# Chunk-end factors kept in a float32 tile and spread by small transfers, one padded v, and a new order, in a gated linear attention that feeds a two-layer MLP

## The chip, the cores and the metric

One core of one Trainium2 chip. The metric is device time in microseconds (us), the median of several runs. The profiler takes one execution apart. The engines are PE (TensorE: matmuls, with PEld for its weight loads), DVE (VectorE), ACT (ScalarE), POOL (GpSimd) and SP (SyncE, which here only issues transfers).

## The reference

The first half is a gated linear recurrence for 4 batches, 8 heads, 768 steps and head dimension 48; the second is a two-layer MLP on the result (3072 tokens, 384 to 2048 to 384).

```python
f = 1.0 / (1.0 + np.exp(-f_logit))
for t in range(S):
    state = f[:, :, t, :, None] * state + np.einsum('bhd,bhe->bhde', k[:, :, t], v[:, :, t])
    y[:, :, t] = np.einsum('bhd,bhde->bhe', q[:, :, t], state)
...
h = x @ w_in
g = np.maximum(0.01 * h, h)
return (g @ w_out).astype(np.float32)
```

## The kernel before

**Units and chunks.** The sequence is cut into 6 chunks of 128 steps, and the work into 12 units, each of 256 tokens. Units 0 to 3 are "paired": unit j holds chunks 0 and 1 of batch j, two neighbouring steps of one chunk pair in a row of 128. Units 4 to 11 hold one chunk (2, 2, 3, 3, 4, 4, 5, 5) of two batches each. The two halves of a unit are called a = 0 and a = 1.

**The steps of a unit**, by the short names that the order uses:

- `Lf Lk Lq Lv` load raw f, k, q, v (192 KB a half; in units 4 and on in runs of 48 floats), by SP's queue. `WI WO` load the MLP's weights in eight pieces each into raw buffers of units 4 and 5 that are still free, and `ci co` cast them to bfloat16.
- `ge gl` on ACT give log of the gate: exp into a tile `e`, then ln(1 + e) into `lf` (L233, L245).
- `cs` on PE sums `lf` over the steps of the chunk (a triangular matmul, L254, L255 in paired units, L262 in the others). The sum of the whole chunk is also wanted down the partitions, one value for each feature: eight matmuls per unit against a column of ones give it (L265; L259 with `half_ones` in paired units). The last chunk (units 10 and 11) needs none.
- `dec` on ACT makes three tiles from these sums: `em` = exp(+) for k, `at` = exp(-) for q, both bfloat16, and `end`, 4 columns in float32 (L273, L274, L276 or L279).
- `k`, `q` scale raw k by `em` and raw q by `at` (L285, on DVE or POOL). In paired units PE transposes them (`tk tq`, L319) and ACT or DVE copies them out (`ck cq`). In units 4 and on SP issues a DMA transpose for each (`xk xq`, L339), which waits until the scaling is done.
- `sc` scores (L355, L362), `mk` four masked copies on DVE (L372, L376), `mx` the mix with v and with the state of the earlier chunk (L393), `ms` its second part in paired units, `xt` copies the result out as input of the MLP.
- `v` casts raw v to bfloat16 (L291) and then copies 16 columns of each head once more into a tile `v2` (L297, L300), so that the mix has 32-column pieces that lie across two heads.
- `pt` (k times v), `sf` on DVE adds it to the float32 state, `sb` on POOL multiplies the state by `end` (L488) and casts it (L491). The state that `sb` of one unit gives is read by `mx` two units later.
- `up`: 6 matmuls of 256 columns (L499) and `pr` on ACT, the leaky relu (L504); 8 for each unit. `dn`: 4 matmuls of 384 columns (L520), 8 for each unit; `ob` copies out, `st` stores. The last unit's second half goes by half the columns (`dc`, L542).
- `F_n_cols` issues n matmuls of zeros (L97); `Z..` and `M..` clear tiles and make constants.

**What sets the order.** The function runs through a string of words such as `up_4_7@2` (step, unit, number, and after the @ its PSUM banks). Each engine takes its instructions in the order of the words and waits in that order; SP's transfers stand in it too. Eight PSUM banks are given out by hand. Raw buffers are six deep, so that unit j's loads wait for unit j-6.

Of the kernel before, what the change touches and what calls it, by code (L numbers as in the profile page):

```python
# [15 lines left out]
def kernel(  # L16
# [14 lines left out]
    C = 128  # L31
# [30 lines left out]
    es = tiles(2, [128, 2, H * D], FP32, "e")  # L62
# [27 lines left out]
    zeros = const.tile([128, 512], BF16, tag="zeros")  # L90
# [16 lines left out]
    def clear_v2(i, e):  # L107
        engine(e).memset(v2s[i][:, :, 1:3, :], 0.0)
# [88 lines left out]
    def load(x, queue=nc.sync):  # L197
        def go(j, a):
            if paired(j):
                h = slice(0, H) if a == 2 else slice(4 * a, 4 * a + 4)  # L200
                queue.dma_start(out=by_pair(raw(j, x))[:, h].rearrange("t h s d -> t h (s d)"),
                                  in_=srcs[x][j, h, 0:2 * C, :].rearrange("h (t s) d -> t h (s d)", s=2))
            else:
                c, h = units[j]
                nc.sync.dma_start(out=raw(j, x)[:, a],
                                  in_=srcs[x][2 * h + a, :, c * C:(c + 1) * C, :].rearrange("h t d -> t h d"))
        return go
# [14 lines left out]
    def decays(j, ts, a):  # L222
        t = ts[j % 2]
# [5 lines left out]
    def gate_e(j, a):  # L229
        e = es[j % 2]  # L230
        src = raw(j, "f").rearrange("t a h d -> t a (h d)")
        part = slice(a, a + 1) if a < 2 else slice(0, 2)
        nc.scalar.activation(e[:, part], src[:, part], AF.Exp, scale=-1.0)  # L233

    def gate_l(j, a):
        e = es[j % 2]
# [10 lines left out]
    def cs(j, a, bank):  # L247
# [15 lines left out]
        if chunk(j, a) < NCH - 1:  # L263
# [4 lines left out]
    def end_of(j):  # L268
        return ends[j % 4]

    def dec(j, a):
        t = banks[st[j]["cs", a]]
        nc.scalar.activation(ems[j % 2][:, a], t[:, 0:H * D], AF.Exp, scale=1.0)  # L273
        nc.scalar.activation(ats[j % 2][:, a], t[:, 0:H * D], AF.Exp, scale=-1.0)  # L274
        if paired(j):
            nc.scalar.activation(end_of(j)[:, :, 2 * a:2 * a + 2].rearrange("t i p -> t p i"),  # L276
                                 t[:, 384:388].rearrange("t (p i) -> t p i", i=2), AF.Exp, scale=-1.0)
        elif chunk(j, a) < NCH - 1:
            nc.scalar.activation(end_of(j)[:, a], t[:, H * D:H * D + P2], AF.Exp, scale=-1.0)  # L279

    def scale(x):
        def go(j, a, e):
            eng = nc.gpsimd if e else nc.vector
            to, by = (khs, ems) if x == "k" else (qhs, ats)
            eng.tensor_mul(heads(j, to[j % NR], a)[:, :, :, 0:D], raw_heads(j, x, a), decays(j, by, a))  # L285
        return go

    def cast_v(j, a, e):
        vb, v2 = vbs[j % 3], v2s[j % 3]
        eng = engine(e)  # L290
        eng.tensor_copy(out=heads(j, vb, a), in_=raw_heads(j, "v", a))  # L291
        if paired(j):
            p = slice(0, P2) if a == 2 else slice(2 * a, 2 * a + 2)
            src = by_pair(raw(j, "v")).rearrange("t (p j) s d -> t j s p d", j=2)
            dst = v2.rearrange("t (s p) n e -> t n s p e", s=2)
            for i in range(2):
                eng.tensor_copy(out=dst[:, 3 * i, :, p], in_=src[:, i, :, p, 32 - 32 * i:48 - 32 * i])  # L297
# [99 lines left out]
    def mix(j, a, *bank):  # L397
# [3 lines left out]
        vb, v2 = vbs[j % 3], v2s[j % 3]  # L401
        jobs = []
        if paired(j):
            halves = range(2) if a == 2 else (a,)
            for s in range(2):
# [7 lines left out]
                for g, which, p, y in todo:  # L413
                    for i in range(2):
                        rows = slice(64 * i, 64 * i + 64)
                        if which == "v":
                            lhsT = vb[rows, s, 2 * p + y, 16 * y:16 * y + 32]
                        else:
                            lhsT = v2[rows, P2 * s + p, 2 * y:2 * y + 2, :]
# [7 lines left out]
        for i in range(2):  # L427
            for y in range(2):
                for p in range(P2):
                    jobs.append((i, 3 * p + 2 * y, vb[:, i, 2 * p + y, 16 * y:16 * y + 32], wm_of(j, i, y)[:, p, :]))  # L430
                for p in range(P2):
                    jobs.append((i, 3 * p + 1, v2[:, P2 * i + p, 2 * y:2 * y + 2, :], wm_of(j, i, y)[:, p, :]))
# [24 lines left out]
    def state(j, a, *bank):  # L457
        kh, vb = khs[j % NR], vbs[j % 3]
        if paired(j):
            for i in range(2):  # L460
                st[j]["pt", i] = bank[i]
            for p in range(P2):
                for s in range(2):
                    for i in range(2):
                        rows = slice(64 * i, 64 * i + 64)
                        nc.tensor.matmul(banks[bank[i]][:, 96 * p:96 * p + 96], kh[rows, s, 2 * p:2 * p + 2, :],
                                         vb[rows, s, 2 * p:2 * p + 2, :], start=(s == 0), stop=(s == 1))
            return
        st[j]["pt", a] = bank[0]
        for p in range(P2):  # L470
            nc.tensor.matmul(banks[bank[0]][:, 96 * p:96 * p + 96], kh[:, a, 2 * p:2 * p + 2, :],  # L471
                             vb[:, a, 2 * p:2 * p + 2, :], start=True, stop=True)

    def state_add(j, a):
        sf = sfs[batch(j, a)]
        pt = banks[st[j].pop(("pt", a))][:, 0:384].rearrange("t (p n) -> t p n", p=P2)
        for y in range(2):
            rows = slice(64 * y, 64 * y + 64)
            new = pt[rows, :, y * D:y * D + D]
            if chunk(j, a) == 0:  # L480
                nc.vector.tensor_mul(sf[rows], new, end_of(j)[rows, a, :, None].to_broadcast([64, P2, D]))  # L481
# [3 lines left out]
    def state_end(j, a):  # L485
        sf, sb = sfs[batch(j, a)], sbs[batch(j, a)][chunk(j, a) % 2]
        if chunk(j, a) > 0:
            nc.gpsimd.tensor_mul(sf, sf, end_of(j)[:, a, :, None].to_broadcast([128, P2, D]))  # L488
# [65 lines left out]
    def store_cols(j, a, h):  # L554
# [12 lines left out]
        "Af": load("f", nc.scalar), "Ak": load("k", nc.scalar), "WI": load_w_in, "WO": load_w_out, "ci": cast_w(w_in_b, 0), "co": cast_w(w_out_b, 8),  # L567
        "Zl": clear_pad(lfs), "Zk": clear_pad(khs), "Zq": clear_pad(qhs), "Zv": clear_v2, "Zb": clear_state,
# [109 lines left out]
```

## Time and profile before

| what | value |
|---|---|
| median of 3 runs | 178.74 us (178.73 to 179.76) |
| the profiled execution's own time | 178.47 us |
| its span, first to last instruction | 176.7 us |
| PE busy | 169.3 us, 96% of the span |
| ACT, DVE, POOL busy | 108.8, 80.3, 77.1 us |
| moved by DMA | 34.44 MB, mean 195 GB/s |

How to read it: a matmul's row has its length with its latency, while PE starts the next one long before that; what PE pays for a piece is read from the chain of waits, where pieces follow each other. A row of the chain has its start, its length and its line. A row of the timeline has start, length, engine, line and operation, with the idle time before it and what ended that in brackets; "SPq" is the time that SP's queue took to issue a transfer. A group's row ends with its count, its busy time in us and the mean of one in ns.

### The profile page before, as it was taken

To read this page: it belongs to the slowest core of one execution; us is meant where nothing else is said; L and a number is where in the kernel's file an instruction comes from. 1 tells how busy PE (TensorE), PEld (TensorE's weight loads), DVE (VectorE), ACT (ScalarE), POOL (GpSimd) and SP (SyncE) were. 2 spreads that over 40 slices of the span, in tenths; PEclk is the share of its full clock that TensorE was granted. 3 is DMA by queue.
4 is the path that set the end of the run, shared out by engine and by line. 5 is a ranking of instruction groups with operands and counts; after the bars stand their busy time and mean duration, and the time that the engine had idled before them with its cause. 6 is when DMAs were issued, how large, how long until landed. Compare 5 with 4: busy or idle time off the path is not lost.

```text
span 176.7 us, 5587 instructions
## 1 busy us (share of the span) xinstructions
PE 169.3 (96%) x2308; PEld 124.5 (70%) x2310; DVE 80.3 (45%) x170; ACT 108.8 (62%) x230; POOL 77.1 (44%) x141
## 2 busy tenths in 40 slices
PE   7698999999999999999999999999999999999993
PEld 2455798688676687767776688777776786788762
DVE  5799797943244644332215750191115843630020
ACT  3995749959846476865683368938882345237511
POOL 7388677540316535255550794274375570000000
PEclk9999999999999999999999999999999999999999
DMA  5999999979983979999999999999989987110013
GB/s 136 323 323 351 325 306 368 329 198 259 233 172 74 188 151 273 179 222 184 210 211 212 222 191 173 203 211 224 157 150 193 166 195 208 46 48 0 4 59 120
DMA packets 108329, 34.44 MB, mean 195 GB/s; under 512 B 101008, under 2 KB 107280, under 8 KB 108304
## 3 DMA queue, kind: packets, MB, share of 16 engines
q1 hardware_dynamic: 107248, 33.70, 82.6%
q10 hardware_dynamic: 1056, 0.39, 0.8%
q8 instruction: 18, 0.29, 0.7%
q14 instruction: 7, 0.06, 0.1%
HBM read 25.17 MB, written 4.72 MB: 169 GB/s over the span
## 4 chain that ended last, share of the span: by engine, by line
PE 87%; DVE 4%; ACT 2%; DMA 2%; issue 1%; POOL 1%; SPq 0%; DVEq 0%; POOLq 0%
PE ps L520 35%; PE ps L499 34%; PE ps L393 6%; PE ps L362 3%; DMA f_raw<-in_f_logit_dram 2%; DVE wm L372 2%; PE ps L319 2%; PE ps L262 2%; PE ps L542 2%; PE ps L355 1%; PE ps L471 1%; DVE kh L285 1%; ACT e L233 1%; PE ps L97 1%; ACT lf L245 1%
## 5 line engine op out<-in xcount | busy, mean ns | idle before, releaser
L504 ACT ACTIVATE gT<-ps 128x512 bf16<-128x512 f32 x96 | 53.1, 608 | 27.1 <-PE ps L499 26.7
L499 PE MATMUL ps<-xT,w_in 128*128 128x256 bf16 x576 | 69.6, 273 | 0.1
L520 PE MATMUL ps<-w_out,gT 128*128 128x384 bf16 x368 | 67.3, 326 | 0.0
L499 PEld LDWEIGHTS <-w_in 128*128 128x128 bf16 x576 | 55.1, 98 | 9.1 <-DVE xT L455 0.4
L520 PEld LDWEIGHTS <-gT 128*128 128x128 bf16 x368 | 34.4, 98 | 19.8
L285 POOL TENSOR_TENSOR qh<-q_raw,at 128x768 bf16<-128x768 f32 (+1 forms) x13 | 18.2, 1398 | 22.0 <-ACT end L279 6.9
L376 DVE TENSOR_TENSOR wm<-ps,ut 128x512 bf16<-128x512 f32 x32 | 20.1, 684 | 10.6 <-PE ps L362 10.5
L273 ACT ACTIVATE em<-ps 128x384 bf16<-128x384 f32 x24 | 11.9, 496 | 19.8 <-PE ps L265 9.3
L483 DVE TENSOR_TENSOR sf<-sf,ps 64x192 f32<-64x192 f32 x32 | 11.2, 349 | 18.0 <-PE ps L471 16.1
L491 POOL CAST sb<-sf 64x192 bf16<-64x192 f32 x40 | 14.5, 362 | 7.4 <-DVE sf L481 5.1
L285 POOL TENSOR_TENSOR kh<-k_raw,em 128x768 bf16<-128x768 f32 (+1 forms) x9 | 14.4, 1602 | 4.9 <-DMA q_raw<-in_q_dram 3.0
L291 POOL CAST vb<-v_raw 128x384 bf16<-128x384 f32 (+1 forms) x13 | 8.8, 676 | 17.3 <-DMA v_raw<-in_v_dram 16.6
L488 POOL TENSOR_TENSOR sf<-sf,end 128x192 f32<-128x192 f32 x16 | 9.1, 572 | 15.0 <-DVE sf L483 14.7
L531 DVE COPY osb<-ps 128x384 f32<-128x384 f32 x13 | 7.2, 554 | 16.1 <-PE ps L520 10.7
L233 ACT ACTIVATE e<-f_raw 128x384 f32<-128x384 f32 (+1 forms) x16 | 11.1, 695 | 2.1 <-DMA f_raw<-in_f_logit_dram 2.0
L372 DVE TENSOR_TENSOR wm<-ps,pair_mask 128x512 bf16<-128x512 f32 x16 | 10.4, 686 | 3.4 <-PE ps L355 3.0
L274 ACT ACTIVATE at<-ps 128x384 bf16<-128x384 f32 x24 | 11.9, 497 | 0.0
L245 ACT ACTIVATE lf<-e 128x384 bf16<-128x384 f32 (+1 forms) x16 | 10.9, 683 | 0.3
L455 DVE CAST xT<-ps 128x384 bf16<-128x384 f32 x11 | 6.1, 566 | 9.8 <-PE ps L393 9.5
L453 ACT CAST xT<-ps 128x384 bf16<-128x384 f32 x13 | 6.6, 526 | 5.5 <-PE ps L393 5.3
L529 ACT COPY osb<-ps 128x384 f32<-128x384 f32 x10 | 4.9, 493 | 6.9 <-PE ps L520 6.9
L97 PE MATMUL ps<-zeros 128*128 128x512 bf16 x20 | 7.8, 467 | 1.4 <-DVE zeros L93 1.2
(92 smaller groups left out, 158.2 us busy)
## 6 DMA issues: line engine op xcount, KB each, us to landing
q_raw<-in_q_dram SPq DMA_DIRECT2D x24, 192.0 KB, 3.8
v_raw<-in_v_dram SPq DMA_DIRECT2D x24, 192.0 KB, 3.6
f_raw<-in_f_logit_dram SPq DMA_DIRECT2D x23, 192.0 KB, 3.9
k_raw<-in_k_dram SPq DMA_DIRECT2D x23, 192.0 KB, 4.5
out_dram<-osb SPq DMA_DIRECT2D x23, 192.0 KB, 2.9
k_raw<-in_moe_w_in_dram SPq DMA_DIRECT2D x2, 384.0 KB, 5.4
f_raw<-in_moe_w_in_dram SPq DMA_DIRECT2D x2, 384.0 KB, 6.5
q_raw<-in_moe_w_in_dram SPq DMA_DIRECT2D x2, 384.0 KB, 6.6
```

Of the source, the lines that this page charges most:

```text
L233: nc.scalar.activation(e[:, part], src[:, part], AF.Exp, scale=-1.0)
L245: nc.scalar.activation(dst, src, AF.Ln, bias=1.0)
L273: nc.scalar.activation(ems[j % 2][:, a], t[:, 0:H * D], AF.Exp, scale=1.0)
L274: nc.scalar.activation(ats[j % 2][:, a], t[:, 0:H * D], AF.Exp, scale=-1.0)
L285: eng.tensor_mul(heads(j, to[j % NR], a)[:, :, :, 0:D], raw_heads(j, x, a), decays(j, by, a))
L372: nc.vector.tensor_mul(w.rearrange("t (s p) n -> t s p n", s=2), src.rearrange("t (s p n) -> t s p n", s=2, p=2), pair_mask[:, :, None, :] ...
L376: nc.vector.tensor_mul(w, src.rearrange("t (p n) -> t p n", p=P2), ut[:, None, :].to_broadcast([128, P2, 128]))
L483: nc.vector.tensor_add(sf[rows], sf[rows], new)
L491: nc.gpsimd.tensor_copy(out=sb[rows, :, y * D:y * D + D], in_=sf[rows])
L499: nc.tensor.matmul(pm[:, i, :], w_in_of(ff, kk), xT_of(j)[:, kk].rearrange("t a s -> t (a s)"), start=(kk == 0), stop=(kk == NK - 1))
L504: nc.scalar.activation(gT_of(j)[:, 2 * g:2 * g + 2, :], pm, AF.Prelu, alpha=0.01)
L520: nc.tensor.matmul(po, gT_of(j)[:, ff, 128 * a:128 * a + 128], w_out_b[ff // 2][:, ff % 2, :], start=(ff == 0), stop=(ff == NF - 1))
```

## The change

1. `at` becomes float32 and holds four more columns for each half, the exponentials of the chunk sums. In paired units one ACT instruction of 388 columns (L311) writes both, and the `end` instruction goes. The tiles `end` of these units are no more; `sf` and `sb` read the columns of `at`.
2. Units 4 to 9 (`SPREAD`) compute no chunk sums by matmul. The last row of their `at` already holds exp(-sum) for each feature, in one partition. Two small transfers for each unit on SP's queue (`xe`, L295; 48 runs of 8 floats each) bring it down the partitions into a tile `end`. For that, `at` of units 4 to 11 is laid out with the eight head pairs innermost: ACT writes and the scaling of q reads with a step of 16 floats.
3. The tile `e` is gone; the first exp is written over raw f.
4. `v` is cast once into a tile with heads padded to 80 columns, whose padding is zero; `v2` and its copies go.
5. The zero matmuls read a tile of 256 columns, twice for 512.
6. The whole order of words is another one, with other banks and other engines for some steps. It has 25 zero matmuls, 4 of them short (22 before), and the first two transfers of ACT's queue are f and v of unit 0 instead of f and k. Changes of shape between neighbouring steps on PE (full, score, mix, paired state) go from 55 to 52.

The diff, cut to its core:

```diff
-    ats = tiles(2, [128, 2, H * D], BF16, "at")
-    ends = tiles(4, [128, 2, P2], FP32, "end")
-    vbs = tiles(3, [128, 2, H, D], BF16, "vb")
-    v2s = tiles(3, [128, 2 * P2, 4, 16], BF16, "v2")
+    SPREAD = (4, 5, 6, 7, 8, 9)
+    ends = tiles(2, [128, 2, P2], FP32, "end")
+    ats = tiles(4, [128, 2 * (H * D + P2)], FP32, "at")
+    VW = D + 32
+    vbs = tiles(3, [128, 2, H, VW], BF16, "vb")
...
-        if chunk(j, a) < NCH - 1:
+        if chunk(j, a) < NCH - 1 and j not in SPREAD:
             for p in range(P2):
                 nc.tensor.matmul(t[:, H * D + p:H * D + p + 1], lf[:, a, 2 * p:2 * p + 2, :], ones_col,
...
+    def at_spread(j):
+        return ats[j % 4][:, 0:2 * H * D].rearrange("t (d y n) -> t n y d", y=2, d=D)
+    def spread_end(j, y):
+        nc.sync.dma_start(out=ends[j % 2][64 * y:64 * y + D].rearrange("d a p -> d (a p)"),
+                          in_=at_spread(j)[C - 1:C, :, y].rearrange("t n d -> t d n"))
...
     def dec(j, a):
         t = banks[st[j]["cs", a]]
         nc.scalar.activation(ems[j % 2][:, a], t[:, 0:H * D], AF.Exp, scale=1.0)
-        nc.scalar.activation(ats[j % 2][:, a], t[:, 0:H * D], AF.Exp, scale=-1.0)
-        if paired(j):
-            nc.scalar.activation(end_of(j)[:, :, 2 * a:2 * a + 2].rearrange("t i p -> t p i"),
-                                 t[:, 384:388].rearrange("t (p i) -> t p i", i=2), AF.Exp, scale=-1.0)
-        elif chunk(j, a) < NCH - 1:
-            nc.scalar.activation(end_of(j)[:, a], t[:, H * D:H * D + P2], AF.Exp, scale=-1.0)
+        if spread(j):
+            nc.scalar.activation(at_spread(j)[:, P2 * a:P2 * a + P2], t[:, 0:H * D].rearrange("t (p y d) -> t p y d", y=2, d=D),
+                                 AF.Exp, scale=-1.0)
+        else:
+            nc.scalar.activation(at_of(j)[:, a], t[:, 0:H * D + P2], AF.Exp, scale=-1.0)
...
     def cast_v(j, a, e):
-        eng.tensor_copy(out=heads(j, vb, a), in_=raw_heads(j, "v", a))
...
+        engine(e).tensor_copy(out=heads(j, vbs[j % 3], a)[:, :, :, 0:D], in_=raw_heads(j, "v", a))
```

Three places of the order show what moves. **PE, unit 4's chunk sums** (`cs_4_0`, `cs_4_1`; `lf` are the gate's logs, `ut` the triangle). Before:

```order
L262 LDWEIGHTS ut_159
L262 MATMUL ps2_147<-lf1_91,ut_159 128x384
L265 LDWEIGHTS lf1_91
L265 MATMUL ps2_147<-ones_col_156,lf1_91 128x1
...
L262 LDWEIGHTS ut_159
L262 MATMUL ps6_151<-lf1_91,ut_159 128x384
```

In the change:

```order
L268 LDWEIGHTS ut_154
L268 MATMUL ps7_147<-lf1_89,ut_154 128x384
L268 LDWEIGHTS ut_154
L268 MATMUL ps4_144<-lf1_89,ut_154 128x384
```

The four loads and four matmuls behind each sum are gone. **ACT, the first steps** (`f_raw0` is unit 0's f, `f_raw1` unit 1's; L332 and L356 copy transposes out). Before:

```order
L233 ACTIVATE e1_89<-f_raw1_65 128x384
L245 ACTIVATE lf1_91<-e1_89 128x4x2x48
L233 ACTIVATE e0_88<-f_raw0_64 128x384
L245 ACTIVATE lf0_90<-e0_88 128x4x2x48
L233 ACTIVATE e0_88<-f_raw0_64 128x384
L245 ACTIVATE lf0_90<-e0_88 128x4x2x48
L273 ACTIVATE em0_99<-ps1_146 128x384
L274 ACTIVATE at0_101<-ps1_146 128x384
L276 ACTIVATE end0_103<-ps1_146 128x2x2
```

In the change:

```order
L239 ACTIVATE f_raw0_64<-f_raw0_64 128x384
L251 ACTIVATE lf0_88<-f_raw0_64 128x4x2x48
L239 ACTIVATE f_raw0_64<-f_raw0_64 128x384
L251 ACTIVATE lf0_88<-f_raw0_64 128x4x2x48
L306 ACTIVATE em0_97<-ps0_140 128x384
L311 ACTIVATE at0_101<-ps0_140 128x388
L306 ACTIVATE em0_97<-ps1_141 128x384
L311 ACTIVATE at0_101<-ps1_141 128x388
L356 COPY kT0_108<-ps2_142 128x2x256
L356 COPY kT0_108<-ps3_143 128x2x256
L239 ACTIVATE f_raw1_65<-f_raw1_65 128x384
```

Unit 0 now goes first and alone; unit 1's gate comes behind unit 0's copies. **SP around unit 7's transposes** (`qh1`, `kh1` are unit 7's scaled q and k in both; `q_raw1` its raw q). Before, with its raw q loaded ten and nineteen transfers earlier:

```order
L339 DMA_TRANSPOSE kT0_113<-kh0_93 128x8x128
L205 DMA v_raw1_83<-in_v_dram 128x8x48
L339 DMA_TRANSPOSE qT1_116<-qh1_97 128x8x128
L339 DMA_TRANSPOSE kT1_114<-kh1_94 128x8x128
L535 DMA out_0_dram<-osb1_142 128x384
```

In the change:

```order
L212 DMA q_raw1_77<-in_q_dram 128x8x48
L557 DMA out_0_dram<-osb0_136 128x384
L295 DMA end0_99<-at2_103 48x1x8 x2
L212 DMA q_raw2_78<-in_q_dram 128x8x48
L557 DMA out_0_dram<-osb2_138 128x384
L212 DMA q_raw1_77<-in_q_dram 128x8x48
L212 DMA k_raw2_72<-in_k_dram 128x8x48
L557 DMA out_0_dram<-osb3_139 128x384
L295 DMA end1_100<-at3_104 48x1x8
L363 DMA_TRANSPOSE kT1_109<-kh1_92 128x8x128
L363 DMA_TRANSPOSE qT1_111<-qh1_95 128x8x128
```

The second half of unit 7's raw q is now loaded three transfers ahead of the first transpose, one of them small.

More of the change, by code (lines that the diff above doesn't have):

```diff
@@ L96, in fill @@
         for _ in range(n):
-            nc.tensor.matmul(banks[bank][:, 0:cols], zeros[:, 0:128], zeros[:, 0:cols], start=True, stop=True)
+            o, src = banks[bank][:, 0:cols], zeros
+            if cols > 256:
+                o, src = o.rearrange("t (a n) -> t a n", n=256), zeros[:, None, :].to_broadcast([128, cols // 256, 256])
+            nc.tensor.matmul(o, zeros[:, 0:128], src, start=True, stop=True)
     def engine(e):
@@ L266, in cs, with spread, at_of, end_of @@
                                  start=True, stop=True)
-    def end_of(j):
-        return ends[j % 4]
+    def spread(j):
+        return not paired(j) and (j in SPREAD or units[j][0] == NCH - 1)
+    def at_of(j):
+        return ats[j % 4].rearrange("t (a n) -> t a n", a=2)
+    def at_spread(j):
+        return ats[j % 4][:, 0:2 * H * D].rearrange("t (d y n) -> t n y d", y=2, d=D)
+    def end_of(j, a, rows=slice(0, 128)):
+        t = ends[j % 2][rows] if j in SPREAD else at_of(j)[rows, :, H * D:H * D + P2]
+        if paired(j):
+            t = t.rearrange("t a (n i) -> t a n i", i=2)[:, :, :, a]
+            return t[..., None].to_broadcast([rows.stop - rows.start, 2, 2, D])
+        return t[:, a, :, None].to_broadcast([rows.stop - rows.start, P2, D])
+    def spread_end(j, y):
+        nc.sync.dma_start(out=ends[j % 2][64 * y:64 * y + D].rearrange("d a p -> d (a p)"),
+                          in_=at_spread(j)[C - 1:C, :, y].rearrange("t n d -> t d n"))
+    def clear_ends(i, e):
+        engine(e).memset(ends[i], 0.0)
+    def like_end(j, t):
+        return t.rearrange("t (a n) d -> t a n d", a=2) if paired(j) else t
     def dec(j, a):
@@ L281, in scale @@
     def scale(x):
         def go(j, a, e):
-            eng = nc.gpsimd if e else nc.vector
-            to, by = (khs, ems) if x == "k" else (qhs, ats)
-            eng.tensor_mul(heads(j, to[j % NR], a)[:, :, :, 0:D], raw_heads(j, x, a), decays(j, by, a))
+            to, by = (khs, ems[j % 2]) if x == "k" else (qhs, ats[j % 4])
+            if x == "q" and spread(j):
+                assert a == 2
+                pairs = lambda t: t.rearrange("t a (p y) d -> t (a p) y d", y=2)
+                engine(e).tensor_mul(pairs(to[j % NR])[:, :, :, 0:D], pairs(raw(j, x)), at_spread(j))
+            else:
+                by = by if x == "k" else at_of(j)
+                engine(e).tensor_mul(heads(j, to[j % NR], a)[:, :, :, 0:D], raw_heads(j, x, a), decays(j, by, a))
@@ L400, in mix @@
             st[j]["py", i] = b
-        vb, v2 = vbs[j % 3], v2s[j % 3]
+        vp = pairs_of_v(vbs[j % 3])
         jobs = []
@@ L415, in mix @@
                         rows = slice(64 * i, 64 * i + 64)
[L416 to L419, printed above, removed]
+                        at = 96 * y if which == "v" else 32 + 32 * y
+                        lhsT = vp[rows, P2 * s + p, at:at + 32]
                         jobs.append((i, g, lhsT, wm_of(j, p // 2, y)[rows, 2 * s + p % 2, :]))
@@ L466, in state @@
                         nc.tensor.matmul(banks[bank[i]][:, 96 * p:96 * p + 96], kh[rows, s, 2 * p:2 * p + 2, :],
-                                         vb[rows, s, 2 * p:2 * p + 2, :], start=(s == 0), stop=(s == 1))
+                                         vb[rows, s, 2 * p:2 * p + 2, 0:D], start=(s == 0), stop=(s == 1))
             return
```

186 lines of the change are left out of this document (88 added, 98 removed).

## The prediction

> **What bounds the kernel now.** I read the page, then the stages, the chain, the timeline of the first 40 us, and SP's timeline.
>
> ```profile
> PE 169.3 (96%) x2308; PEld 124.5 (70%) x2310; DVE 80.3 (45%) x170; ACT 108.8 (62%) x230; POOL 77.1 (44%) x141
> DMA  5999999979983979999999999999989987110013
> ...
> 0.00:10.00 10.00, 7.09 (x48) 3.38 (x48) 6.88 (x25) 7.03 (x17) 5.93 (x27) 1.00 0.89 240
> 10.00:20.00 10.00, 9.03 (x222) 5.95 (x223) 8.80 (x18) 7.22 (x17) 7.58 (x19) 1.00 1.11 341
> ...
> 40.00:60.00 20.00, 20.00 (x235) 13.72 (x233) 8.54 (x20) 13.35 (x31) 6.09 (x9) 1.00 0.85 183
> 60.00:80.00 20.00, 20.00 (x306) 15.33 (x282) 8.77 (x17) 13.98 (x32) 8.81 (x15) 1.00 1.01 207
> ```
>
> From 40 us on PE (second number of a stage) never rests. So time is lost in two ways only: before 40 us, where units 0 to 2 pass from engine to engine and zero matmuls count as busy, and by any new wait later. The row "DMA" says that such a wait has a candidate: transfers are in flight nearly all the time up to about 145 us.
>
> **1. The sums by matmul.**
>
> ```profile
> 50.50 0.16 PE ps L262
> 50.67 0.08 PE ps L265 x4
> 50.75 0.18 PE ps L262
> ...
> 126.14 0.16 PE ps L262
> 126.30 0.66 PE ps L499 x6
> ```
>
> In the chain four L265 take 0.08 us, and a sum of the last chunk, which has none, is followed at once by the next work (126.30). Units 4 to 9 have 12 such groups, on PE, in its dense part: 12 x 0.08 = **-1.0**. It lies between 0.9 and 1.2, as the rows are rounded.
>
> **2. Changes of shape on PE.**
>
> ```profile
> 76.03 1.30 PE ps L520 x8
> 77.33 0.55 PE ps L362 x16
> 77.88 1.41 PE ps L520 x8
> ```
>
> Eight L520 behind a score take 1.41 instead of 1.30: 0.1 for each change of shape. 55 become 52: **-0.3** (-0.4 to 0, as some stand where PE waits anyway).
>
> **3. Work taken from ACT, DVE and POOL.** The `end` steps, the `v2` copies and one clear less are off the path while PE is dense: ACT is busy 13 to 14 of 20 us there, POOL 6 to 9. I cost it at nothing; PE's own work hides it. At the start it counts, below. Writing the first exp over raw f holds that buffer one step longer; its next load comes six units later: nothing.
>
> **4. The start, in the new order.** ACT now gates unit 0 alone, then makes its factors; unit 1 comes behind.
>
> ```profile
> 4.06 0.52 ACT L233 ACTIVATE e<-f_raw 128x384 f32<-128x384 f32 x1 [2.04 <-DMA f_raw<-in_f_logit_dram]
> 7.18 0.47 ACT L273 ACTIVATE em<-ps 128x384 bf16<-128x384 f32 x1
> ...
> 7.28 0.38 ACT em L273
> 7.66 0.38 ACT at L274
> 8.16 0.55 DVE qh L285
> 8.71 0.47 DVE kh L285
> 9.21 0.44 DVE qT L334
> ...
> 15.55 0.31 PE L393 MATMUL ps<-wm,vb 64*32 64x128 bf16 x16
> 26.25 2.79 ACT L504 ACTIVATE gT<-ps 128x512 bf16<-128x512 f32 x5 [0.92 <-PE ps L499]
> 30.19 2.48 DVE L372 TENSOR_TENSOR wm<-ps,pair_mask 128x512 bf16<-128x512 f32 x4 [0.48 <-PE ps L355]
> ```
>
> A walk along the queues with these lengths (rows of the chain are from start to start): gate of unit 0 from 4.06, two pairs at about 1.05, done 6.2; factors, four steps, done 7.9 (before, three pairs came first: 7.18 is the first factor). DVE: q, k, q, v, two copies, `sf`, four masks: done about 13.5, so unit 0's mix at 13.6 instead of 15.55. But unit 1 pays: its k on DVE stands behind these masks, POOL makes q, v and k of its second half one after the other (13.6 to 16.4), and its four masks, mixed with `sf` and a weight cast, end at about 22.2. Three `up` groups fill PE before its mix, where before there was one. Behind it the relus (2.79 for five, 0.56 each) pace PE up to the end of unit 2's mix, which I put at 36.6. PE has then done the work that the kernel before has done here:
>
> ```profile
> 37.07 0.25 PE L254 MATMUL ps<-lf,bu 128*128 128x192 bf16 x1
> 37.23 0.08 PE ps L254
> ```
>
> In both, 23.35 us at the chain's prices (0.65 for each `up` or `dn`, and so on: 15 `up` and 3 `dn` there, 14 and 4 here, all else alike). So **-0.6** (37.2 to 36.6). The walk has some 30 handovers; 0.05 us on each would take it to +0.9, and with unit 1's masks not in the way it could be -1.5.
>
> **5. The small transfers and what they stand among.** Their price has no row. The nearest small one is a 96 KB store:
>
> ```profile
> out_dram<-osb SPq DMA_DIRECT2D x2, 96.0 KB, 1.6
> q_raw<-in_q_dram SPq DMA_DIRECT2D x24, 192.0 KB, 3.8
> qT<-qh SPq DMA_TRANSPOSE x8, 3.8
> ...
> 174.07 0.33 SPq L557 DMA_DIRECT2D out_dram<-osb  x1
> ```
>
> So 1.6 to 3.8 to land and 0.33 (or less, or up to a load's 1 us) of SP's time; I take 0.3 for 48 short runs. `sb` waits for them, but `sb`'s result is read two units later, over 14 us on: hidden. What is not hidden is the queue:
>
> ```profile
> 55.89 1.23 SPq L339 DMA_TRANSPOSE kT<-kh  x1
> 57.21 0.53 SPq L205 DMA_DIRECT2D q_raw<-in_q_dram  x1
> ...
> 91.24 1.67 SPq L339 DMA_TRANSPOSE qT<-qh  x1
> 142.44 1.21 SPq L205 DMA_DIRECT2D v_raw<-in_v_dram  x2
> ...
> 99.91 0.55 PE ps L362 x16
> ```
>
> From 57.21 to 143.65 SP issues 54 loads, 13 transposes and 15 stores without a long rest. At 1.35 and 0.6 for the latter two that leaves 1.1 us for a load with SP's waits in it, about 1.0 without. Before, the transpose of unit 7's q was issued at 91.24, landed about 95.0, and the scores ran at 99.91. In the new order SP stops at unit 0's first store, then unit 4's q and k are scaled on POOL, and the second transpose issues at 58.6; then come 27 loads, 7 stores, 4 transposes and 6 small transfers up to the second half of unit 7's raw q: 58.6 + 27 + 4.2 + 5.4 + 1.8 = 97.0, landed 99.8. POOL's scaling follows, then the transpose:
>
> ```profile
> L285 POOL TENSOR_TENSOR qh<-q_raw,at 128x768 bf16<-128x768 f32 x8 | 13.2, 1651 | 18.2 <-ACT end L279 6.9 <-ACT at L274 4.1 <-ACT gT L504 2.9
> L488 POOL TENSOR_TENSOR sf<-sf,end 128x192 f32<-128x192 f32 x16 | 9.1, 572 | 15.0 <-DVE sf L483 14.7
> ```
>
> It now reads `at` in float32 with a step. Bounds: 1.65 as before, and 2.3 by the float32 product of L488 (572 x 4). 99.8 + 1.65 to 2.3 + 3.8 = 105.2 to 105.9. PE comes there after 91.4 us of its work (all steps ahead of it at the chain's prices), 13.2 behind (36.6 - 23.35): 104.6. Two places ahead are as tight by the same count: unit 4's scores (transpose landed 60.7, PE there at 60.3) and unit 5's `up`, whose relus stand behind four long gate steps: 0.3 each. So PE is at unit 7's scores at 105.2 and waits 0 to 0.7; I take 0.4. Together **+1.0**; 0 if loads go a little faster, 5 if they take 1.1 and the small transfers more.
>
> [...] No run here shows such a step; the row of 1651 is without one. ACT writes with the same step; its row is 0.38 and twice that would still be hidden, as ACT has 6 of 20 us free.
>
> **Sum**, against the profiled execution's 178.47 (span 176.7 and 1.8 around it): -1.0 - 0.3 - 0.6 + 1.0 = -0.9, so **177.6 us**. That execution is 0.3 below the median of the runs shown, 178.74.
>
> **Rivals.**
>
> - *The start gains more and the queue keeps up.* With -1.5 at the start and no wait: 178.47 - 1.0 - 0.3 - 1.5 = 175.7. For it: the first mix has two us in hand, and SP rests before unit 4 with loads done. Against: DVE and relus set the pace from 14 to 33 us in my walk.
> - *The transfers become the bound (slower).* One place decides: unit 7's raw q. If a load takes 1.1 us and a small transfer 0.5 of SP's time, it lands 2.7 + 1.2 = 3.9 later, and PE waits 0.4 + 3.9 there. With the other terms 178.47 - 1.9 + 0.6 + 4.3 = 181.5. From about 1.06 us a load the time is above that of before. For it: the row of DMA and 1.1 as the mean with waits; against: 1.1 counts SP's rests twice.
> - *The small transfers hold up the state.* `dec` of unit 8 overwrites `at` of unit 4 and so waits for its second small transfer, which stands behind a transpose on SP; ACT would stop, its relus too. By my count it has 1.5 us in hand; if it is 3 us late, 177.6 + 1.5 = 179.1.
> - *The order does nothing*: the start is as long as before and the waits come: 178.47 - 1.3 + 1.0 = 178.2.
>
> **How the numbers follow.** My sum and the last two rivals lie within 1% of the median, which is what a measurement of this kernel can tell from no change (176.95 to 180.5): 0.42 together. The first rival, with the part of my own case under 176.95: 0.35. The slow one, beyond 180.5: 0.23, as loads must go slower than they did without SP's rests. The range reaches from 175.2, half a us under the first rival, to 181.2, most of the way to the slow one; my own case alone is 176.6 to 178.9.
>
> **What would show it.** Right: no matmul against ones behind units 4 to 9; unit 0's mix before 14.5; PE at work without a break from about 24; POOL's q of units 4 and on at 1.65 to 2.3; unit 7's scores preceded by an idle PE of about 1 us or less, released by a DMA transpose. Wrong: a wait of over 2 us on PE behind 40 us, a first dense `up` later than 26, or PE's dense part no shorter than before.

## The result and the profile after

The change made the kernel slower by about 1%: 182.31 us (median of 20 runs, 179.71 to 183.85) against 179.35 for the kernel before, run beside it; the ratio is 1.0107, 95% interval 1.0076 to 1.0137. The ratio leaves out runs that lie over 1.5% above a kernel's fastest, so it is smaller than that of the medians. Two more measurements of the same change, below, gave 181.05 (1.0094) and 181.59 (1.0118).

The profiled execution took 182.88 us, with a span of 181.0 (before: 178.47 and 176.7). From its page, the engines' busy time, the granted clock, and the two groups with the step:

```profile
PE 171.3 (95%) x2265; PEld 125.1 (69%) x2265; DVE 78.7 (44%) x161; ACT 113.9 (63%) x211; POOL 77.8 (43%) x127
...
PEclk9999999999999999999999996999999999999999
...
L319 POOL TENSOR_TENSOR qh<-q_raw,at 128x768 bf16<-128x768 f32 x8 | 17.6, 2195 | 10.3 <-DMA q_raw<-in_q_dram 7.0
...
L308 ACT ACTIVATE at<-ps 128x384 f32<-128x384 f32 x16 | 13.5, 841 | 0.0
```

PE does less work than before (2265 matmuls for 2308) and is busy longer; one slice has a clock of 0.6. The scaling of q on POOL went from 1.65 to 2.2 us, ACT's write of `at` from 0.50 to 0.84.

The start came nearly as forecast. In the chain of waits the last piece of unit 2's mix ends at 36.7; the kernel before had done the same work on PE at 37.2, the row of L254 in the prediction:

```profile
35.70 1.02 PE ps L417 x73
36.73 5.35 PE ps L521 x48
...
77.46 0.60 ACT gT L526
78.06 0.13 SPq L295
...
83.98 3.52 DMA f_raw<-in_f_logit_dram
87.53 0.85 ACT f_raw L239
...
105.25 3.29 DMA qT<-qh
108.53 0.14 issue
108.67 0.62 PE ps L386 x16
109.29 5.01 PE ps L542 x20
```

In the kernel before, the chain stays on PE through the whole dense part. Here it leaves PE twice: from 77 to 95 it runs over a small transfer (L295) and SP's loads to unit 7's f, to ACT's gate and the relus behind it; and at 105.25 over a DMA transpose to unit 7's scores (L386). What PE waited for from 40 us on (in all, times, longest), and then the stretch around the second place: its length, the busy time of PE, PEld, DVE, ACT and POOL, the granted clock, DMA's share and GB/s:

```profile
PE ps L386 <- DMA qT<-qh: 1.9, 1, 1.9
PE ps L521 <- ACT gT L526: 0.5, 1, 0.5
PE ps L542 <- ACT gT L526: 0.3, 1, 0.3
```

```profile
104.00:108.00 4.00, 2.78 (x24) 2.01 (x21) 0.56 (x1) 3.72 (x8) 3.09 (x5) 1.00 0.66 124
108.00:110.00 2.00, 1.33 (x19) 0.91 (x20) 0.84 (x2) 0.88 (x2) 2.00 (x2) 0.80 0.99 191
110.00:112.00 2.00, 2.00 (x8) 0.91 (x6) 2.00 (x4) 0.00 (x0) 1.06 (x1) 0.50 1.14 226
112.00:114.00 2.00, 2.00 (x12) 1.11 (x11) 0.11 (x1) 0.00 (x0) 0.00 (x0) 0.85 1.20 246
```

From one matmul's start to the next, beyond the usual distance of its kind, PE loses 0.64 us at 89.0 and 0.43 at 94.2 (waits for relus) and 2.05 at 106.5 (the scores). The down matmuls behind that rest start 0.32 us apart instead of 0.16: the clock column gives 2 x (0.20 + 0.50 + 0.15) = 1.7 us lost.

SP's queue and POOL show why the scores waited. SP's rows (L212 a load, L295 small transfers, L363 a transpose), then POOL's scaling of unit 7's q:

```profile
96.22 1.18 SPq L295 DMA_DIRECT2D end<-at  x2
97.44 0.58 SPq L212 DMA_DIRECT2D q_raw<-in_q_dram  x1
98.12 0.52 SPq L557 DMA_DIRECT2D out_dram<-osb  x1
98.69 0.43 SPq L212 DMA_DIRECT2D q_raw<-in_q_dram  x1
...
102.50 1.28 SPq L363 DMA_TRANSPOSE kT<-kh  x1
105.25 1.23 SPq L363 DMA_TRANSPOSE qT<-qh  x1
```

```profile
103.03 2.19 POOL L319 TENSOR_TENSOR qh<-q_raw,at 128x768 bf16<-128x768 f32 x1 [5.76 <-DMA q_raw<-in_q_dram]
```

The second half of unit 7's raw q is issued at 98.69; POOL has waited 5.76 us for it when it starts at 103.03. A small transfer takes SP 0.6 us (1.18 for the pair above), as much as a load of 192 KB (0.58 and 0.43).

**The account** of the profiled executions, span for span: start -0.5; sums -1.24 (48 matmuls, 26 ns from start to start each); other prices of PE's work +0.4; rests +3.1; half clock +1.7; from PE's last matmul to the end 3.8 instead of 3.2, +0.55; the remaining 0.3 in small rests, 0.2 of it in unit 3's mix at 59.7. Together 4.3 = 181.0 - 176.7.

### The profile page after: what moved, and what is told of

It reads as the page before. It is cut to its first block, busy times and chain, and to the rows that moved or that the text cites. A ratio compares the mean times of both kernels' runs of the same rounds, so it can differ in the third digit from the quotient of the medians.

```text
span 181.0 us, 5487 instructions
## 1 busy us (share of the span) xinstructions
PE 171.3 (95%) x2265; PEld 125.1 (69%) x2265; DVE 78.7 (44%) x161; ACT 113.9 (63%) x211; POOL 77.8 (43%) x127
## 4 chain that ended last, share of the span: by engine, by line
PE 77%; DMA 6%; DVE 5%; ACT 5%; SPq 3%; issue 2%; POOL 0%; ACTq 0%; DVEq 0%
PE ps L521 32%; PE ps L542 30%; PE ps L417 5%; DMA f_raw<-in_f_logit_dram 4%; SPq L212 2%; PE ps L386 2%; DMA qT<-qh 2%; ACT gT L526 2%; PE ps L564 1%; PE ps L343 1%; PE ps L268 1%; DVE wm L396 1%; DVE qh L322 1%; PE ps L493 1%; DVE qT L358 1%
## 5 line engine op out<-in xcount | busy, mean ns | idle before, releaser
L521 PE MATMUL ps<-xT,w_in 128*128 128x256 bf16 x576 | 67.1, 273 | 0.6 <-ACT gT L526 0.5
L526 ACT ACTIVATE gT<-ps 128x512 bf16<-128x512 f32 x96 | 54.6, 607 | 17.8 <-PE ps L521 15.5
L319 POOL TENSOR_TENSOR qh<-q_raw,at 128x768 bf16<-128x768 f32 x8 | 17.6, 2195 | 10.3 <-DMA q_raw<-in_q_dram 7.0
L326 POOL CAST vb<-v_raw 128x384 bf16<-128x384 f32 (+1 forms) x9 | 6.8, 758 | 20.5 <-DMA v_raw<-in_v_dram 13.4
L308 ACT ACTIVATE at<-ps 128x384 f32<-128x384 f32 x16 | 13.5, 841 | 0.0
L510 POOL TENSOR_TENSOR sf<-sf,end 128x192 f32<-128x192 f32 x12 | 6.1, 506 | 16.4 <-DVE sf L505 10.1
L239 ACT ACTIVATE f_raw<-f_raw 128x384 f32<-128x384 f32 (+1 forms) x16 | 10.9, 690 | 3.6 <-DMA f_raw<-in_f_logit_dram 3.6
L251 ACT ACTIVATE lf<-f_raw 128x384 bf16<-128x384 f32 (+1 forms) x16 | 10.8, 682 | 0.4
L322 POOL TENSOR_TENSOR qh<-q_raw,at 128x384 bf16<-128x384 f32 x3 | 3.5, 1160 | 14.9 <-ACT at L311 14.9
L100 PE MATMUL ps<-zeros 128*128 128x512 bf16 (+1 forms) x25 | 8.5, 457 | 1.1 <-DVE zeros L93 1.1
```

The source lines that it names most:

```text
L239: nc.scalar.activation(e[:, part], e[:, part], AF.Exp, scale=-1.0)
L308: nc.scalar.activation(at_spread(j)[:, P2 * a:P2 * a + P2], t[:, 0:H * D].rearrange("t (p y d) -> t p y d", y=2, d=D), AF.Exp, scale=-1.0)
L319: engine(e).tensor_mul(pairs(to[j % NR])[:, :, :, 0:D], pairs(raw(j, x)), at_spread(j))
L322: engine(e).tensor_mul(heads(j, to[j % NR], a)[:, :, :, 0:D], raw_heads(j, x, a), decays(j, by, a))
L521: nc.tensor.matmul(pm[:, i, :], w_in_of(ff, kk), xT_of(j)[:, kk].rearrange("t a s -> t (a s)"), start=(kk == 0), stop=(kk == NK - 1))
L526: nc.scalar.activation(gT_of(j)[:, 2 * g:2 * g + 2, :], pm, AF.Prelu, alpha=0.01)
```

## Experiments

Ratios are to the kernel before, run beside each; the interval is 95%.

| kernel | median us | ratio | interval |
|---|---|---|---|
| q7_early | 180.38 | 1.0072 | 1.0038 to 1.0105 |
| g7_behind | 180.90 | 1.0097 | 1.0067 to 1.0127 |
| q7_g7 | 179.79 | 1.0044 | 1.0018 to 1.0069 |
| sums_back | 179.17 | 1.0003 | 0.9986 to 1.0020 |
| no_transfers | 179.30 | 1.0022 | 0.9995 to 1.0049 |
| transfers_unread | 179.57 | 1.0036 | 1.0003 to 1.0070 |
| old_order_sums | 179.45 | 1.0029 | 1.0002 to 1.0056 |
| old_order_spread | 184.30 | 1.0317 | 1.0258 to 1.0375 |
| change_again | 181.05 | 1.0094 | 1.0057 to 1.0131 |
| ends_on_act | 184.16 | 1.0297 | 1.0266 to 1.0327 |
| ends_on_act_v7 | 184.36 | 1.0300 | 1.0262 to 1.0339 |
| no_ends | 178.22 | 0.9972 | 0.9944 to 0.9999 |
| half_runs | 180.94 | 1.0097 | 1.0057 to 1.0137 |
| change_third | 181.59 | 1.0118 | 1.0087 to 1.0148 |
| act_stride | 178.76 | 0.9976 | 0.9954 to 0.9998 |
| sums_v7 | 178.63 | 0.9957 | 0.9937 to 0.9978 |

### Is it the place of the loads? q7_early, g7_behind, q7_g7

Words of the order; `Lq_7_1` loads half of unit 7's raw q, `ge_7 gl_7` are its gate steps on ACT.

```diff
-    q_6_2_1 xq_6 Lk_8_0 Lk_7_1 Lf_9_0 Lq_8_0 Lf_9_1 Lq_7_0
+    q_6_2_1 xq_6 Lq_7_1 Lk_7_1 Lf_9_0 Lq_7_0 Lf_9_1 Lq_8_0
...
-    up_5_6@1 pr_5_6 Lq_7_1 up_5_4@2
+    up_5_6@1 pr_5_6 Lk_8_0 up_5_4@2
```

> The changed kernel with four loads of SP's queue in each other's places: the two halves of unit 7's raw q go where half of unit 8's k and half of unit 8's q stood, six and nine transfers earlier, and those take their places. Theory A (unit 7's q is late because of where its loads stand in SP's queue): the idle 2.05 us of PE before unit 7's scores and the 1.7 us that the down matmuls behind it lose to a half clock go; 182.3 - 3.7 = 178.6, PE idle at unit 7's scores under 0.3. Rival B (transfers as such are the bound; whatever goes first, something else is as late): the wait comes back at unit 8's scores or unit 9's gate, 181 to 182.3. Rival C (the strided scaling and the small transfers make q late, not the loads): within 0.5 of the changed kernel.

Measured 180.38. The wait before unit 7's scores is gone, as A said, but others came, 2.6 us in all from start to start, with those that were there:

```profile
PE ps L521 <- DVE osb L553: 0.7, 1, 0.7
PE ps L417 <- DVE wm L400: 0.3, 1, 0.3
PE ps L521 <- ACT gT L526: 0.3, 1, 0.3
PE ps L542 <- ACT gT L526: 0.3, 1, 0.3
```

PE is at the next place sooner, and there an output copy (`osb`), the last mask or v's cast is not ready. The time lies between the forecasts, and its interval overlaps that of the change (1.0038 to 1.0105, 1.0076 to 1.0137). So moving the loads removes the wait before unit 7's scores, but gains little time.

```diff
-    Lf_7_0 ge_7_2 gl_7_2 k_6_2_1
+    Lf_7_0 k_6_2_1
...
-    up_5_0@7 pr_5_0 pt_5_0@4
+    up_5_0@7 pr_5_0 ge_7_2 gl_7_2 pt_5_0@4
```

> The changed kernel with ACT's two gate steps of unit 7 moved behind unit 5's first four relus. Under A the 0.64 and 0.43 us that PE waits for these relus at 89 and 94 go, but PE only comes sooner to unit 7's scores, which wait for the same transfer: no change, 181.9 to 182.6, the wait at unit 7's scores longer by about 1 us. Rival (each wait of PE counts for itself): 182.3 - 1.1 = 181.2.

Measured 180.90; its ratio, 1.0097, is that of the change: no gain, as A said. The rest before unit 7's scores is still there (2.08 us). It did not grow, since another 0.64 came at unit 7's sums, which now waited for the gate that was moved.

> Both edits: unit 7's raw q earlier and its gate steps behind unit 5's first relus. Theory A: both waits go, 182.3 - 3.7 - 1.1 = 177.5, below the kernel before by 1%. Rival B: 181 or more, with a new wait on a transfer.

Measured 179.79: by the ratios 0.6% under the change (intervals 1.0018 to 1.0069 and 1.0076 to 1.0137), but 2.3 above A's number, with rests of 0.64 at unit 7's sums, 1.0 at an output copy and 0.86 in unit 7's mix. Mending one wait at a time runs into the next.

### Is it the spread itself? sums_back

```diff
-    SPREAD = (4, 5, 6, 7, 8, 9)
+    SPREAD = ()
...
-    st_0_1 ob_2_1_0 xe_4_0 Lv_4_0 st_1_1
+    st_0_1 ob_2_1_0 Lv_4_0 st_1_1
```

(and the other `xe` words)

> The changed kernel, its order as it is, but the chunk sums of units 4 to 9 by matmul again: no small transfers, at of these units contiguous. PE gains 12 sums at 0.08 (+1.0). SP has 12 small transfers less, six of them (3.8 us of its time by the profile of the changed kernel) ahead of unit 7's second half of raw q; ACT's write goes from 0.84 to 0.50 and POOL's scaling from 2.2 to 1.65. If the small transfers and the stride are what makes q late (C), the waits of 5.1 go: 182.3 - 5.1 + 1.0 = 178.2. If the place of the loads alone does it (A), part of the wait stays: 180 to 181. If neither matters (B): 183.3.

Measured 179.17, level with the kernel before. PE pays for the sums again and all waits over 0.5 us are gone. SP's rows for unit 7, second half of q and both transposes:

```profile
94.82 0.43 SPq L212 DMA_DIRECT2D q_raw<-in_q_dram  x1
...
97.59 1.29 SPq L363 DMA_TRANSPOSE kT<-kh  x1
100.46 1.23 SPq L363 DMA_TRANSPOSE qT<-qh  x1
```

The load is 3.9 us sooner, which is the 3.8 of SP's time that six small transfers ahead of it took in the change (0.62 + 1.46 + 0.55 + 1.18); the q transpose is 4.8 sooner. The measured time is nearest to C, though 1.0 above its number; A alone and B don't fit.

### Transfers or stride? no_transfers, transfers_unread, no_ends, act_stride

no_transfers drops the 12 `xe` words and nothing else.

> The changed kernel without its 12 small transfers: the tile that they fill stays at zero, so the state of units 4 to 9 is multiplied by zero and not by the chunk ends; all else, the strided at and the strided scaling too, is as in the change, and no sums by matmul. sums_back took away transfers and stride at once; this takes the transfers alone. If the transfers hold SP up (theory T): unit 7's second half of raw q issues about 3.9 us sooner, as there (94.8 instead of 98.7), the wait before unit 7's scores is gone, and the time is that of sums_back less the sums, 179.2 - 1.2 = 178.0 (177.5 to 178.6). If the stride does it (theory S: ACT's writes of 0.84 and POOL's scaling of 2.2 make the chain late): unit 7's scores still wait 1 us or more, 180 or more.

Measured 179.30. SP's rows for unit 7's q:

```profile
95.03 0.43 SPq L212 DMA_DIRECT2D q_raw<-in_q_dram  x1
...
101.16 1.24 SPq L363 DMA_TRANSPOSE qT<-qh  x1
```

The load goes 3.7 us sooner than in the change, the transpose 4.1, and the scores don't wait: without the transfers most of the loss is gone. But 178.0 was missed by 1.3, so something else costs as well; the next runs look at the stride.

transfers_unread is sums_back with the `xe` words back in their places.

> sums_back (sums by matmul, at contiguous) with the 12 small transfers issued all the same, at their places in the change; nobody reads what they bring. T: the wait at unit 7's scores comes back in great part, as the second half of unit 7's raw q issues at about 98 again; the stride's share of it (POOL's scaling 0.55 shorter) is missing; 181 to 182.5. S: as sums_back, 179.2 (up to 179.7).

Measured 179.57, a miss: I put the wait too high. SP is held up as in the change, but less comes of it:

```profile
97.69 0.43 SPq L212 DMA_DIRECT2D q_raw<-in_q_dram  x1
...
103.79 1.23 SPq L363 DMA_TRANSPOSE qT<-qh  x1
```

The q transpose goes at 103.79: 3.3 later than in sums_back, 1.5 sooner than in the change. PE, with the sums to do, arrives at about 105.9 and rests 1.0. (The list of waits names ACT's factors here, which end at 106.9 like the transpose's landing; in sums_back the scores ran before those factors were done, so it is the transpose.) The costs add up along one queue against a slack: with the transpose at 101.2 nothing is lost, at 103.8 it is 1.0, at 105.25 it is 2.05 and in some executions the clock.

no_ends makes `at` of units 4 to 9 contiguous, without sums and transfers:

```diff
-        return not paired(j) and (j in SPREAD or units[j][0] == NCH - 1)
+        return not paired(j) and units[j][0] == NCH - 1
...
```

> no_transfers with at of units 4 to 9 contiguous again (the tile of the ends stays at zero here too): neither sums, transfers nor stride in these units, that is, the order with the chunk ends for nothing. Against no_transfers it prices the stride alone: 0.5 less (178.8) if ACT's 0.35 and POOL's 0.55 for each show only where PE waited in that profile (0.24 at unit 3's transposes, 0.4 at unit 7's mix); 179.3 if the stride is hidden altogether. Against sums_back it prices the sums: 1.2 less, 178.0, if PE is the bound all along.

Measured 178.22. Against sums_back the sums cost 0.95 us by the medians and 1.1 by the profiled spans (177.2 and 176.1). Against no_transfers the stride costs 0.5%, 0.9 us, by the ratios (0.9972 and 1.0022; their intervals just touch), and 0.8 by the spans (176.9 and 176.1): most of what dropping the sums gains, the stride alone takes away.

act_stride keeps ACT's strided writes and lets POOL read the tile contiguously:

```diff
-            if x == "q" and spread(j):
+            if x == "q" and spread(j) and j not in SPREAD:
...
```

> no_transfers (ends zero) with ACT's writes of at strided as before, but POOL's scaling of q reading the tile contiguously (so q is scaled by the wrong elements). It lies between no_ends (178.2, no stride) and no_transfers (179.3, both). ACT pays 0.34 for each of 16 writes, POOL 0.55 for each of 6 scalings. If the relus that stand behind the writes carry the stride's price: 179.3. If q's late transposes do: 178.2 to 178.5.

Measured 178.76, which neither forecast had: by the median it lies half way between no_ends (178.22) and no_transfers (179.30), by the ratio (0.9976) at no_ends, and the intervals can't decide. The profiles can. All three kernels issue the same matmuls in the same order, so their starts on PE can be laid side by side. The spans are 176.1, 176.5 and 176.9, and each of the two steps has its place.

ACT's strided write costs 0.38. Each half of unit 4's `at` takes 0.81 instead of 0.48. PE's transposes of unit 3 go to PSUM banks that this write, and an output copy behind it on ACT, must first have read, so they come 0.24 later (those of q at 53.66 for 53.42); another 0.09 comes at 79.5.

POOL's strided reading costs 0.43, of which 0.38 at one place, and not through a transpose of q. POOL's scaling of unit 8's q runs beside DVE's cast of unit 7's v. In act_stride:

```profile
107.67 1.81 POOL L322 TENSOR_TENSOR qh<-q_raw,at 128x768 bf16<-128x768 f32 x1
```

```profile
107.81 2.09 DVE L326 CAST vb<-v_raw 128x768 bf16<-128x768 f32 x1
```

In no_transfers these two take 2.19 and 2.47 (rows in the last section): DVE's cast ends 0.4 us behind POOL's step in both. The mix of unit 7 waits for the cast, and its first matmul with v starts at 110.38 instead of 109.96.

### By the issue or by the run? half_runs, change_third

```diff
-        nc.sync.dma_start(out=ends[j % 2][64 * y:64 * y + D]...
-                          in_=at_spread(j)[C - 1:C, :, y]...
+        nc.sync.dma_start(out=ends[j % 2][64 * y:64 * y + D // 2]...
+                          in_=at_spread(j)[C - 1:C, :, y, 0:D // 2]...
```

> The changed kernel with small transfers of 24 runs instead of 48: they bring the ends of the first 24 features of each head alone (the other rows of the tile stay zero). If a small transfer is paid by the issue, 0.6 us of SP each however little it brings: as the changed kernel beside it, 181 to 182.3. If it is paid by the run: SP's time for one falls to about 0.3, unit 7's raw q issues about 1.9 us sooner, and the time lies half way to no_transfers, 180 to 180.7.

> The changed kernel beside half_runs, for the comparison: 181.0 to 182.3, as in its two measurements.

Measured 180.94 and 181.59, ratios 1.0097 and 1.0118 with intervals that overlap widely. Half the runs save SP nothing:

```profile
96.55 1.51 SPq L295 DMA_DIRECT2D end<-at  x2
...
102.97 0.75 SPq L295 DMA_DIRECT2D end<-at  x1
```

These took 1.18 and 0.51 with all 48 runs (1.16 for the pair in change_third, beside it). The price is by the issue.

### On another queue: ends_on_act, ends_on_act_v7, change_again

```diff
-        nc.sync.dma_start(out=ends[j % 2][64 * y:64 * y + D]
+        nc.scalar.dma_start(out=ends[j % 4][64 * y:64 * y + D]
```

Each pair of `xe` words stands behind its unit's second `dec`; there are four tiles of ends.

> The changed kernel itself, beside the others on the same chip: 182.3 (181.5 to 183). It also shows whether the half clock behind the rest before unit 7's scores (11 down matmuls of 0.32 in its profile, 0.16 in that of g7_behind after the same rest) comes again.

> The changed kernel with the 12 small transfers on ACT's queue, each pair right behind its unit's factors (four tiles for the ends, so that none waits for an older one's reader); SP issues none. Output as the reference. Theory T (the small transfers cost SP about 0.6 us each, as much as a load, and six of them stand ahead of unit 7's raw q): as no_transfers, 179.3 (178.6 to 179.8), unit 7's scores with less than 0.3 of idle PE. Theory Q (they hold up the DMA engines or the readers of the ends wait for them, whichever queue issues them): 181 or more. If ACT pays 0.6 for each and that reaches the relus: 180 to 180.5.

Measured 184.16, worse than the change. Unit 7's scores no longer wait, but PE comes to them 4.6 us later than in no_transfers (110.18 for 105.55), so that alone shows nothing. SP's rows do: it issues the second half of unit 7's q at 95.84 and its transpose at 102.98 (95.03 and 101.16 in no_transfers, 98.69 and 105.25 in the change). The transfers are all still made and hold up SP's loads no more, as T said and against Q. But ACT pays, far more than the 180.5 that I had for that:

```profile
53.27 1.22 ACTq L295 DMA_DIRECT2D end<-at  x2
54.52 1.25 ACT L551 COPY osb<-ps 128x384 f32<-128x384 f32 x3 [1.29 <-PE ps L343]
...
71.06 1.86 ACTq L295 DMA_DIRECT2D end<-at  x2
72.96 0.86 ACT L475 CAST xT<-ps 128x384 bf16<-128x384 f32 x2 [1.93 <-issue]
...
82.34 1.16 ACTq L295 DMA_DIRECT2D end<-at  x2
83.55 0.60 ACT L526 ACTIVATE gT<-ps 128x512 bf16<-128x512 f32 x1 [1.24 <-issue]
```

A pair takes ACT 1.2 to 1.9 us, and behind it stand output copies, x's copy and relus. PE waited for exactly these:

```profile
PE ps L521 <- ACT xT L475: 1.7, 1, 1.7
PE ps L343 <- ACT osb L551: 1.4, 1, 1.4
PE ps L542 <- ACT gT L526: 1.3, 1, 1.3
```

The price moved with the issue, from a queue with some slack to an engine with none at those places.

> ends_on_act, and unit 7's raw v loaded between its two transposes, where SP rests 2 us in the profile of no_transfers, instead of behind them. There the mix of unit 7 waited 0.4 for v's cast. T: ends_on_act less 0.4 to 0.9 (178.2 to 178.8), below before. Rival: the loads go ahead of the q transpose in the DMA engines and make it late: unit 7's scores wait, no gain.

184.36, the same three waits: the edit for unit 7 could not show here.

### The order and the spread apart: old_order_sums, old_order_spread

Both have the code of the change and the words of before; the second with `xe_j_0 xe_j_1` behind each unit's later transpose.

> The code of the change in the order of before, with the sums by matmul: one padded v, exp written over raw f, ends inside at of float32, denser zero matmuls; no small transfer, no stride but in units 10 and 11. In the dense part this work is hidden behind PE; at the start it shortens DVE, ACT and POOL by some 0.5 us in all. 178.6 to 179.3. Rival: at in float32 makes the scaling of q slower on DVE at the start and eats what is saved: 179.3 to 179.8.

> old_order_sums with the small transfers in place of the sums of units 4 to 9, each pair issued behind its unit's later transpose (five tiles for the ends instead of two, so that no transfer waits for an older one's reader). PE saves 1.2 of sums. In this order the raw q and k of unit 7 are loaded nine transfers or more ahead, so T forecasts that the small transfers find slack: old_order_sums less 1.2, about 177.8. Rival: they stand in front of loads here too, and the 0.6 us of SP's time for each make a later load late: no gain, or slower, 179 to 181.

old_order_sums took 179.45: the rest of the change's code, in the old order, is 0.3% slower than before (interval 1.0002 to 1.0056), as the rival there had it. Its scaling of q on DVE, with `at` in float32, is 702 ns a piece instead of 583. Against it sums_back, with the new order, is 0.26% faster, 0.5 us, which would be the order's gain and close to the -0.6 of the start; the intervals overlap (1.0002 to 1.0056, 0.9986 to 1.0020), so it is likely and not shown.

old_order_spread took 184.30, where I expected 177.8 and the rival 179 to 181. The pairs stand in front of loads and stores there too, and a store that is late holds an output tile, for which ACT waits with relus behind it, and PE for ACT:

```profile
82.44 0.48 ACT L551 COPY osb<-ps 128x384 f32<-128x384 f32 x1 [3.19 <-DMA out_dram<-osb]
```

```profile
PE ps L521 <- ACT osb L551: 4.3, 2, 2.5
PE ps L386 <- DMA kT<-kh: 1.0, 1, 1.0
```

My nine transfers of slack for unit 7's q did not help the stores. The new order bears the small transfers better than the old one.

### A version below both: sums_v7

```diff
-    k_7_2_1 xk_7 dn_5_1_1
+    k_7_2_1 xk_7 Lv_7_1 Lv_7_0 dn_5_1_1
...
-    Lv_7_1 sc_7_2@1.4.3.5 mk_7_0_0 mk_7_1_1 mk_7_1_0 Lv_7_0 v_7_2_0 mk_7_0_1
+    v_7_2_0 sc_7_2@1.4.3.5 mk_7_0_0 mk_7_1_1 mk_7_1_0 mk_7_0_1
```

This edit is made to sums_back.

> sums_back, with unit 7's raw v loaded between its two transposes and its cast ahead of unit 7's masks on DVE. In the profile of sums_back PE waited 0.47 in unit 7's mix for the last mask, which stood behind that cast. If that rest goes: 178.7, below the kernel before by 0.3%. Rival: the loads push the q transpose, unit 7's scores wait, 179.2 or more.

Measured 178.63, ratio 0.9957 (0.9937 to 0.9978): behind 24 us PE has no rest over 0.2, and the kernel is 0.4% below the one before, with the new order, the single padded v and the sums by matmul.

## Why the prediction was wrong

- **The sums by matmul**, -1.0: right. 1.24 by PE's starts, 0.95 by the medians (sums_back less no_ends).
- **Changes of shape**, -0.3: came to nothing. The starts of `up` stand 0.28 us closer in all, but from a state product (L493, 48 of them) to PE's next matmul it is 54 ns instead of 44 in the mean, +0.4. Among themselves these start 43 ns apart in both kernels, so it is what stands behind them that costs.
- **Work taken from ACT, DVE and POOL**, 0: that work was hidden, but the new layout's own price was not. I had twice ACT's row as still hidden, and counted POOL's longer scaling of q for unit 7's transpose alone. The strided write costs 0.38 at unit 3's transposes, the strided reading 0.43 in unit 7's mix, by way of DVE's cast of v: together 0.8 of the 1.1 us that the sums save in the same profiles.
- **The start**, -0.6: right in size (36.7 against 37.2), and unit 0's mix began at 13.6 as forecast.
- **The small transfers and what they stand among**, +1.0: this is the step that failed: 3.1 us of rests came. Unit 4's scores did not wait (I had 0.3). Unit 5's `up` waited at the place named, behind the gate steps, 0.64 and a further 0.43 instead of 0.3. Unit 7's scores waited 2.05 instead of 0.4. There I took 0.3 us of SP's time for a small transfer, arguing from 48 short runs and a 96 KB store; it is 0.6, and no less with half the runs. Six of them make 2.0 (3.8 less 1.8) of the 2.1 us by which the load was late, 99.1 instead of 97.0 at the end of its issue; it then took 3.9 us to POOL's start at 103.03, about 1 more than I took. POOL's 2.2 lay within my bounds, the transpose's 3.3 was shorter than my 3.8.
- **POOL's strided reads.** The scaling takes 2.2 us with the step of 16 floats; contiguous, with `at` in float32, it takes 1.82 in act_stride. So the step costs 0.38 us, a fifth, and the rest of the growth from 1.65, 0.17, comes with float32.
- **Not in the sum at all**: 1.7 us of half clock behind the rest, and 0.55 at the end of the program.

The transfers are not the whole miss. Without them (no_transfers) no wait stands before unit 7's scores, and my other terms would give -1.9; yet its profiled span is 176.9, 0.2 above that of before. The start and the sums brought their 0.55 and 1.24. Against them stand the 0.2 that the change of shapes cost in place of -0.3, the stride's 0.8, a rest of 0.5 for unit 7's last mask, the one of 0.2 in unit 3's mix and 0.34 at the end.

The slow rival had this mechanism, this place and a small transfer at 0.5, and gave 181.5. I gave it a chance of 0.23, since I held that it needed slower loads as well; the loads went as I had taken them, and the small transfers alone made q late. Most of its wait (2.7 of 3.9) was to come from the loads, so that its number lies near the measured one is in part luck. My bounds for one went from 0.3 or less to a load's 1 us, and I took the lower end for the sum. The rival of the held-up state did not come: unit 8's factors follow the relus at 92 without a wait for a transfer. What the page's share of DMA and the chain could not tell is which of the two, SP's issue or the transfers' bytes, sets the pace; no_transfers and half_runs show that it is the issue.

The sign that I named for being wrong, a wait of over 2 us on PE behind 40, is the 2.05 before unit 7's scores, behind the row of 105.25.

## What to carry to other kernels

Here a small transfer was paid on the queue that issued it, by the issue: about 0.6 us of SP's time each (3.8 for the six ahead of unit 7's q), 0.6 to 0.9 of ACT's (1.2 to 1.9 a pair). Before it replaces work of a busy engine, add its measured price to that queue and see what stands behind it there, loads, stores and, on a computing engine, its own steps. Weigh what the new layout costs the readers as well: here 0.8 of the 1.1 us gained on PE was spent by a strided operand before any transfer was counted. Where several delays share one slack, each alone seems cheap (transfers_unread lost 0.4), and together they are not.

## What the runs showed of the hardware

DVE's cast of unit 7's v takes 0.56 us in sums_v7, where it goes at 103.60, ahead of the masks; where it starts 0.13 to 0.14 us behind POOL's scaling of unit 8's q it takes 2.09 (act_stride) and 2.47 (no_transfers); a row of DVE and one of POOL in no_transfers, then DVE's in sums_v7:

```profile
107.86 2.47 DVE L326 CAST vb<-v_raw 128x768 bf16<-128x768 f32 x1
```

```profile
107.73 2.19 POOL L319 TENSOR_TENSOR qh<-q_raw,at 128x768 bf16<-128x768 f32 x1
```

```profile
103.60 0.56 DVE L326 CAST vb<-v_raw 128x768 bf16<-128x768 f32 x1 [2.17 <-DMA v_raw<-in_v_dram]
```

The cast began 0.13 us after POOL's step and ended 0.4 after it (110.33 and 109.92), as it did in act_stride behind a shorter step (109.90 and 109.48), so it looks as if it had run behind it, not beside it. This is how a longer step of POOL reached PE. What holds the cast back was not shown.

The half clock came in two of three profiles of the change (0.50 for 2 us above; 0.57 for 4 us in change_again), in that of half_runs, and not in the change's third, nor in g7_behind, where PE rested as long before the same scores:

```profile
108.00:110.00 2.00, 1.53 (x22) 1.08 (x23) 1.05 (x2) 0.65 (x1) 2.00 (x2) 1.00 1.07 211
110.00:112.00 2.00, 2.00 (x15) 1.22 (x13) 1.91 (x4) 0.00 (x0) 0.83 (x1) 1.00 1.03 198
```

PE's wait before these scores was as long with the half clock as without it: by the list of waits 1.9 us in the first two profiles of the change and 1.8 in that of half_runs, 1.9 in the change's third and in g7_behind. So its length alone does not decide, and what does was not shown. Over a whole program 1.7 us lost is a mean clock of 0.99: of the change's 33 executions in its three measurements 8 have 0.989 to 0.991 and the others 0.996 or more, so the 1.7 us of the account belong to about one execution in four. In sums_back and no_transfers none of 24 has it; in old_order_spread, where the longest wait is 2.5 us, 5 of 6; in old_order_sums, where the longest behind 24 us is 0.3, 3 of 12 have 0.990.
